# Moving x of chunk 1 and the v weights one wave earlier, with a newly searched order of steps, in a fused attention and MLP kernel

## The chip, the cores and the metric

One core of a Trainium2 chip. The metric is the device time of one launch in microseconds (us), lower is better. Profiles give a span that is about 2 us shorter than the time of the same run (201.3 and 203.08 us before, 204.6 and 206.41 changed). Every run is in the state that the records call fast. For one core the records also give the mean granted clock of TensorE (1.0 is full speed), which matters below.

## The reference

x has 2048 rows of 512. The block is: layer norm, q, k and v projections, attention of 32 heads of 16 over eight positions two apart (a row's own and seven earlier ones), an output projection with residual (this sum is h), layer norm of h, a gated MLP of 1376 hidden columns, and again a residual.

```python
off = jnp.arange(8) * 2
idx = pos[:, None] - off[None, :]            # each row looks at 8 rows, 2 apart
logits = jnp.einsum("bhsd,bhswd->bhsw", q, kg) * scale
attn = softmax(where(mask, logits, -1e9))
o = jnp.einsum("bhsw,bhswd->bhsd", attn, vg)
h = x + o @ wo
g = layernorm(h) @ W_gate
out = h + (g * (g > 0) * (layernorm(h) @ W_up)) @ W_down
```

## The kernel before

The rows are worked on in four chunks of 512 (chunk 0 to 3), which overlap. All steps are put in a list, and a table `RANK` gives each its place; each engine is given its steps in that order. The table was searched off the chip with assumed durations. The loads come first, in waves: a later wave is held back by a one-element copy on GpSimd that reads the earlier one and writes into the later one's tile (the first such copy runs at 3.61 us, and x of chunk 1 is issued at 3.81).

```python
for j in range(BPC):                                  # x of chunk 0: four blocks, on two queues
    (nc.scalar if j % 2 else nc.sync).dma_start(x_sm[:, j:j + 1, :], x_rows[:, j:j + 1, :])
for dt in range(NT):                                  # q and k weights: four slices, on two queues
    (nc.scalar if dt % 2 else nc.sync).dma_start(wqk_sb[:, dt:dt + 1, :], w3_r[:, dt:dt + 1, 0:2 * D])
# ... constants ...
nc.gpsimd.tensor_copy(out=x_sm[0:1, BPC, 0:1], in_=x_sm[0:1, 0, 0:1])          # gate
nc.sync.dma_start(x_sm[:, BPC:2 * BPC, :], x_rows[:, BPC:2 * BPC, :])           # x of chunk 1
nc.gpsimd.tensor_copy(out=wv_sb[0:1, 0, 0:1], in_=wqk_sb[0:1, NT - 1, 0:1])    # gate
nc.sync.dma_start(wv_sb[:], w3_r[:, :, 2 * D:3 * D])                            # v weights
nc.gpsimd.tensor_copy(out=x_sm[0:1, 2 * BPC, 0:1], in_=x_sm[0:1, BPC, 0:1])    # gate
# ... x of chunks 2 and 3, then wo, up, gate, down weights
```

Normalised rows are transposed before the products with the weights. Most are transposed on TensorE itself; those in `DMAT` by a DMA on the SP queue, one for each block of 128 rows: all four of x of chunk 3, two of h of chunk 1, all of h of chunks 2 and 3.

```python
DMAT = (('h',2,0),('h',2,2),('x',3,0),('x',3,2),('h',3,0),('h',3,2),('h',1,0))
# in layernorm(): xn is a normalised block
nc.sync.dma_start_transpose(out=dst.t[:, :, j * P:(j + 1) * P], in_=xn.t[:])
```

The sum over eight positions of attention times v is begun with a DMA too. After a v product on VectorE (128x4096, 2.2 us from start to start), an accumulating transfer of 512 KB, issued from GpSimd, adds its second half to its first. There are four of these in each of chunks 0, 1 and 2.

```python
def f_da(mt=mt):
    nc.gpsimd.dma_start(mt.t[:, 0:4, :], mt.t[:, 4:8, :], accum_op=ALU.add)
```

In the names used below, `xxn` is the normalising of one block of x on VectorE, `xtd` its transpose by DMA, `mu` a v product, `hxn` the normalising of a block of h.

The softmax here doesn't subtract the row's maximum and nothing guards it: scores larger than these inputs give would overflow.

Of the kernel before, what the change touches and what calls it, by code (L numbers as in the profile page):

```python
# [17 lines left out]
RANK = [  # L18
    0, 1, 2, 3, 4, 5, 6, 7, 8, 9, 10, 11, 12, 13, 14, 15, 16, 18, 19, 24,
    26, 31, 32, 17, 20, 22, 23, 25, 29, 34, 35, 28, 33, 37, 39, 41, 45, 48, 21, 27,  # L20
    30, 36, 38, 42, 44, 46, 63, 74, 40, 56, 68, 49, 51, 54, 43, 60, 72, 53, 66, 65,
    77, 70, 83, 75, 80, 90, 92, 87, 114, 102, 110, 85, 105, 93, 104, 115, 125, 129, 78, 88,
    95, 99, 103, 183, 193, 202, 132, 143, 150, 156, 152, 106, 109, 116, 123, 119, 168, 181, 216, 220,
    224, 180, 188, 217, 223, 231, 187, 196, 226, 229, 234, 162, 172, 201, 205, 207, 237, 240, 239, 245,
    247, 251, 242, 248, 243, 246, 252, 256, 259, 263, 250, 254, 265, 266, 272, 278, 269, 276, 285, 275,
    283, 273, 280, 286, 318, 322, 292, 301, 304, 314, 313, 324, 341, 311, 325, 298, 303, 334, 338, 326,
    330, 346, 354, 360, 337, 355, 317, 353, 347, 358, 370, 329, 352, 340, 348, 332, 345, 294, 350, 356,
    361, 374, 343, 365, 372, 381, 351, 362, 413, 357, 368, 367, 386, 418, 400, 425, 460, 464, 417, 427,
    457, 467, 376, 434, 446, 466, 410, 429, 437, 668, 55, 61, 52, 57, 50, 58, 47, 59, 62, 64,
    67, 84, 73, 82, 86, 71, 81, 69, 79, 89, 166, 175, 122, 136, 111, 130, 137, 190, 91, 101,  # L30
    127, 173, 149, 179, 94, 96, 163, 213, 158, 170, 98, 107, 108, 167, 208, 197, 249, 257, 244, 235,
    255, 260, 264, 268, 274, 296, 279, 302, 309, 305, 310, 307, 287, 295, 290, 293, 300, 319, 328, 364,
    369, 315, 320, 359, 363, 335, 342, 380, 382, 327, 336, 373, 375, 389, 395, 387, 392, 396, 402, 393,
    399, 398, 401, 397, 403, 405, 409, 404, 407, 411, 412, 416, 419, 420, 423, 421, 428, 422, 426, 431,
    474, 482, 441, 443, 458, 463, 453, 468, 483, 438, 448, 436, 452, 442, 451, 450, 454, 456, 488, 492,
    479, 498, 455, 487, 491, 500, 507, 461, 493, 445, 459, 481, 485, 471, 475, 496, 511, 539, 524, 533,
    520, 535, 526, 530, 541, 514, 540, 484, 502, 543, 544, 556, 581, 589, 538, 552, 559, 562, 549, 554,
    584, 587, 529, 547, 560, 564, 113, 120, 100, 124, 76, 117, 97, 112, 128, 133, 140, 144, 142, 146,
    164, 145, 154, 148, 157, 161, 209, 230, 174, 186, 198, 200, 195, 215, 182, 184, 199, 228, 189, 211,
    169, 177, 178, 194, 232, 241, 271, 281, 185, 191, 261, 253, 284, 297, 289, 282, 308, 312, 321, 331,  # L40
    339, 344, 378, 366, 377, 371, 379, 383, 385, 394, 388, 391, 390, 430, 439, 470, 490, 424, 432, 473,
    476, 440, 447, 486, 489, 406, 415, 465, 477, 501, 518, 497, 504, 508, 512, 494, 499, 521, 525, 517,
    519, 516, 522, 503, 505, 527, 528, 532, 546, 534, 537, 536, 548, 531, 542, 579, 597, 566, 594, 585,
    601, 561, 580, 609, 599, 603, 588, 592, 571, 575, 577, 600, 605, 606, 610, 595, 623, 602, 611, 582,
    614, 627, 558, 576, 574, 578, 568, 572, 565, 567, 583, 621, 648, 639, 645, 636, 649, 591, 616, 652,
    624, 635, 628, 633, 640, 655, 663, 665, 667, 632, 654, 661, 711, 650, 656, 707, 710, 644, 657, 659,
    669, 126, 138, 118, 134, 131, 139, 121, 135, 141, 147, 155, 160, 151, 171, 159, 165, 153, 176, 203,
    236, 218, 225, 192, 204, 214, 219, 258, 291, 262, 270, 222, 233, 267, 277, 227, 238, 212, 221, 288,
    316, 206, 210, 306, 299, 323, 333, 384, 349, 408, 414, 433, 435, 444, 462, 449, 506, 510, 509, 513,
    515, 469, 495, 478, 472, 480, 563, 570, 586, 593, 523, 551, 557, 569, 573, 590, 596, 598, 545, 550,  # L50
    553, 555, 615, 622, 604, 607, 612, 619, 608, 613, 626, 629, 618, 620, 630, 631, 617, 625, 634, 637,
    638, 641, 646, 653, 643, 651, 642, 647, 691, 695, 681, 692, 694, 698, 688, 697, 700, 679, 687, 674,
    677, 670, 680, 666, 671, 690, 673, 675, 672, 682, 658, 662, 660, 678, 683, 684, 689, 664, 685, 699,
    702, 676, 693, 705, 701, 706, 704, 709, 686, 703, 708, 713, 715, 716, 718, 696, 714, 719, 720, 722,
    724, 731, 712, 726, 732, 734, 717, 725, 727, 730, 728, 733, 735, 737, 721, 723, 729, 736,
]


# [33 lines left out]
class Plan:  # L92
# [9 lines left out]
    def add(self, key, *a, **k):  # L102
        op = Op(*a, **k)
        op.key = key
        op.seq = len(self.ops)
        if RANK:
            op.prio = RANK[op.seq]
        self.ops.append(op)
        for b in set(op.take) | set(op.use):
            b.left += 1  # L110
        return op
# [76 lines left out]
def kernel(  # L188
# [11 lines left out]
    nc = tc.nc  # L200
# [4 lines left out]
    NT = D // P  # L205
# [11 lines left out]
    BPC = CS // P  # L217
# [4 lines left out]
    x_rows = A_x.rearrange("b (tb p) d -> p (b tb) d", p=P)  # L222
# [20 lines left out]
    x_sm = sb.tile([P, NTB, D], BF16, name="x_sm")  # L243
    wqk_sb = sb.tile([P, NT, 2 * D], BF16, name="wqk_sb")
    wv_sb = sb.tile([P, NT, D], BF16, name="wv_sb")
# [32 lines left out]
    def setup():  # L278
# [3 lines left out]
            (nc.scalar if j % 2 else nc.sync).dma_start(x_sm[:, j:j + 1, :], x_rows[:, j:j + 1, :])  # L282
        for dt in range(NT):
            (nc.scalar if dt % 2 else nc.sync).dma_start(wqk_sb[:, dt:dt + 1, :], w3_r[:, dt:dt + 1, 0:2 * D])
        nc.scalar.preload_act_table_set("natural_log_exp_and_others")
        V.memset(warm[:], 0.0)
        make_identity(nc, identity[:])
# [7 lines left out]
        nc.gpsimd.memset(vT[:, :, 0:PADL], 0.0)  # L295


        nc.gpsimd.tensor_copy(out=x_sm[0:1, BPC, 0:1], in_=x_sm[0:1, 0, 0:1])
        nc.sync.dma_start(x_sm[:, BPC:2 * BPC, :], x_rows[:, BPC:2 * BPC, :])
        nc.gpsimd.tensor_copy(out=wv_sb[0:1, 0, 0:1], in_=wqk_sb[0:1, NT - 1, 0:1])  # L300
        nc.sync.dma_start(wv_sb[:], w3_r[:, :, 2 * D:3 * D])
        nc.gpsimd.tensor_copy(out=x_sm[0:1, 2 * BPC, 0:1], in_=x_sm[0:1, BPC, 0:1])
        for tk in range(2, NCK):
# [32 lines left out]
    DAL = 5.5  # L336
    TDD, TDL = 1.25, 1.5
    NWARM, NFILL = 44, 8
    DMAT = (('h',2,0),('h',2,2),('x',3,0),('x',3,2),('h',3,0),('h',3,2),('h',1,0))

    EARLY = (1, 2, 3)

# [20 lines left out]
    def load(t):  # L363
        return add(None, "LD", 0.0, None, lat=t)

    xload = [[load(t) for t in (3.4, 3.4, 4.2, 4.2)]] + [[load(t)] * BPC for t in (9.5, 14.0, 15.5)]
    wload = {n: load(t) for n, t in
             (("q", 8.0), ("k", 8.0), ("v", 12.0), ("o", 17.5), ("u", 21.5), ("g", 25.5), ("d", 29.5))}

    wb = Buf(bank_s)  # L370

# [14 lines left out]
    def layernorm(tk, src, dst_slots, pr, groups, on_act, residual=None):  # L386
# [7 lines left out]
        for grp in groups:  # L394
# [72 lines left out]
            for j0 in range(lo, hi, step):  # L467
                if (ln, tk, j0) in DMAT:
                    for j in range(j0, min(j0 + step, hi)):
# [38 lines left out]
    for tk in range(NCK):  # L508
# [143 lines left out]
        for t in range(NT):  # L652
# [18 lines left out]
            if (tk, t) in PESUM:  # L671
                u = Buf(od_s)
# [66 lines left out]
        for f0 in range(0, NFT, 2):  # L739
# [3 lines left out]
            for ft in fts:  # L743
# [20 lines left out]
                d = add(("ge%d" % (f0 // 2), tk), "ACT", A5, f_ge, [c], pr - 200, take=[gr], use=[gm], lat=AL)  # L764
# [50 lines left out]
    with tc.manual_schedule():  # L815
        setup()
        for op in todo:
            if op.fn is not None:
                op.fn()
# [35 lines left out]
```

## Time and profile before

| | before |
|---|---|
| time, first 3 runs | 204.51 us (204.45 to 204.53) |
| profiled run | 203.08 us, span 201.3 us |
| TensorE busy | 194.4 us, 97% |
| VectorE busy | 153.1 us, 76% |
| x of chunk 1 issued, landed | 3.81, 9.91 us |
| v weights issued, landed | 8.85, 13.38 us |

Timelines have the start in us, the busy time, engine and line, operation, output and inputs, count, and in brackets the idle time of the engine before the line with what ended it. SPq is the SP queue issuing a transfer. This is the view of waits of TensorE in the kernel before (what waited, for what, us in total, times, longest):

```profile
...
PE bank L525 <- DMA quad<-row: 0.7, 1, 0.7
...
PE bank L525 <- DMA wqk_sb<-in_A_wqkv_dram: 0.6, 1, 0.6
PE bank L750 <- DMA quad<-row: 0.4, 1, 0.4
```

`quad<-row` is a transposed block. TensorE waits once for those of x of chunk 3, once for those of h of chunk 1, and once for the q and k weights. Idle time is a little less than time lost, since the modelled end of the last matmul lies after the start of the next: the twelve v matmuls at 16.92 us count as 2.75 us busy, and the next group starts 2.59 us after their start. I therefore give lost time as the distance between two starts minus the work of the first (2.59 us for twelve is 0.216 us for one of 512 columns), as the prediction works it out.

### The profile page before, as it was taken

Reading aid. Unit: us, or ns where it says so; the run is one execution under the profiler, and the core shown is the slowest. Engines: PE = TensorE matmul, PEld = TensorE weight load, DVE = VectorE, ACT = ScalarE, POOL = GpSimd, SP = SyncE. Lnnn points to the kernel's source line nnn. Section 1 sums busy time; section 2 is a strip of 40 time slices with the busy share of each in tenths; the row PEclk is TensorE's granted clock in tenths of the full one; section 3 lists DMA queues with packets and bytes.
Section 4 is the critical chain, followed back from the end, with each engine's and each line's share of the span. In section 5 each row is a group of like instructions: output and inputs, shape, how many; then the busy total and the mean of one; then the engine's idle time right before and its main releaser. Section 6 shows DMA issues by size and latency. Waiting matters only on the chain.

```text
span 201.3 us, 2960 instructions
## 1 busy us (share of the span) xinstructions
PE 194.4 (97%) x1115; PEld 96.0 (48%) x1115; DVE 153.1 (76%) x239; ACT 121.9 (61%) x256; POOL 12.8 (6%) x29
## 2 busy tenths in 40 slices
PE   8799999989999999999999999999999999999993
PEld 8676445545445344434444444444444444444452
DVE  6778999999999999999995858799967412122313
ACT  3377699746899966787536679801566731277500
POOL 3000000420000013100122000000000000000000
PEclk9999999999999999999999999999999999999999
DMA  5799971896000008930299500131010050200103
GB/s 152 270 256 379 406 219 41 155 205 122 3 0 0 3 0 169 190 57 3 39 182 191 138 3 0 26 78 52 3 52 0 0 104 3 78 0 0 52 0 104
DMA packets 17676, 18.81 MB, mean 93 GB/s; under 512 B 8352, under 2 KB 14464, under 8 KB 17664
## 3 DMA queue, kind: packets, MB, share of 16 engines
q1 hardware_dynamic: 15360, 11.57, 18.7%
q0 software_dynamic: 1728, 6.29, 16.8%
q10 hardware_dynamic: 576, 0.79, 1.3%
q8 instruction: 8, 0.13, 0.3%
q14 instruction: 4, 0.03, 0.0%
HBM read 8.42 MB, written 2.10 MB: 52 GB/s over the span
## 4 chain that ended last, share of the span: by engine, by line
PE 55%; DVE 24%; DMA 11%; ACT 5%; issue 2%; SPq 1%; POOL 0%; DVEq 0%; ACTq 0%; POOLq 0%
PE bank L750 29%; PE bank L787 14%; DVE big L572 7%; DMA x_sm<-in_A_x_dram 7%; DVE big L660 7%; PE bank L525 6%; PE bank L712 5%; DMA quad<-row 4%; DVE st L420 2%; DVE row L455 2%; DVE gT L770 2%; DVE x_sm L723 1%; DVE big L663 1%; ACT big L645 1%; ACT row L409 1%
## 5 line engine op out<-in xcount | busy, mean ns | idle before, releaser
L750 PE MATMUL bank<-quad,wg_sb 128*128 128x512 bf16 (+1 forms) x176 | 42.5, 379 | 0.4 <-DMA quad<-row 0.4
L750 PE MATMUL bank<-quad,wu_sb 128*128 128x512 bf16 (+1 forms) x176 | 42.7, 379 | 0.1
L757 ACT ACTIVATE gr<-bank 128x512 bf16<-128x512 f32 (+1 forms) x44 | 25.4, 618 | 24.8 <-PE bank L750 23.0
L787 PE MATMUL bank<-wd_sb,gT 128*128 128x512 bf16 (+3 forms) x187 | 40.0, 367 | 0.0
L754 ACT CAST up_sb<-bank 128x512 bf16<-128x512 f32 (+1 forms) x44 | 25.1, 601 | 21.0 <-PE bank L750 19.3
L572 DVE TENSOR_TENSOR big<-quad,kT 128x4096 bf16<-128x4096 bf16 x16 | 36.2, 2283 | 0.1
L660 DVE TENSOR_TENSOR big<-big,vT 128x4096 bf16<-128x4096 bf16 x16 | 35.9, 2281 | 0.0
L770 DVE TENSOR_TENSOR gT<-gr,up_sb 128x1024 bf16<-128x1024 bf16 (+1 forms) x24 | 15.3, 642 | 24.0 <-ACT up_sb L754 14.4
L525 PE MATMUL bank<-quad,wqk_sb 128*128 128x512 bf16 (+1 forms) x144 | 30.6, 356 | 1.3 <-DMA quad<-row 0.7
L787 PEld LDWEIGHTS <-gT 128*128 128x128 bf16 (+1 forms) x187 | 18.1, 98 | 19.6 <-issue 0.4
L750 PEld LDWEIGHTS <-wg_sb 128*128 128x128 bf16 (+1 forms) x176 | 17.3, 100 | 21.3 <-issue 0.9
L750 PEld LDWEIGHTS <-wu_sb 128*128 128x128 bf16 (+1 forms) x176 | 17.5, 100 | 20.6 <-issue 0.7
L525 PEld LDWEIGHTS <-wqk_sb 128*128 128x128 bf16 x144 | 15.5, 114 | 13.5 <-issue 2.2
L798 DVE TENSOR_TENSOR row<-x_sm,bank 128x512 bf16<-128x512 bf16 (+1 forms) x17 | 10.6, 649 | 10.4 <-PE bank L787 10.4
L645 ACT CAST big<-bank 128x512 bf16<-128x512 f32 x32 | 17.8, 638 | 0.4 <-PE bank L639 0.4
L663 DVE TENSOR_TENSOR big<-big 128x1024 bf16<-128x1024 bf16 (+2 forms) x24 | 16.8, 728 | 0.1
L692 POOL DMA_DIRECT2D big<-big x12 | 10.5, 872 | 87.9 <-DVE big L660 59.8
L525 PE MATMUL bank<-quad,wv_sb 128*128 128x512 bf16 x64 | 15.7, 380 | 0.0
L712 PE MATMUL bank<-wo_sb,quad 128*128 128x512 bf16 x64 | 15.3, 379 | 0.0
L455 DVE TENSOR_SCALAR row<-x_sm,mv,rs 128x512 bf16<-128x512 bf16 x32 | 11.3, 407 | 3.1 <-ACT rs L437 3.1
L533 ACT CAST quad<-bank 128x512 bf16<-128x512 f32 x16 | 9.4, 609 | 4.5 <-PE bank L525 4.5
L500 ACT COPY quad<-bank 128x1024 bf16<-128x1024 bf16 (+1 forms) x9 | 8.0, 930 | 6.3 <-PE bank L484 6.2
(69 smaller groups left out, 146.7 us busy)
## 6 DMA issues: line engine op xcount, KB each, us to landing
big<-big POOLq DMA_DIRECT2D x12, 512.0 KB, 5.5
out_dram<-row SPq DMA_DIRECT2D x15, 128.0 KB, 1.8
x_sm<-in_A_x_dram SPq DMA_DIRECT2D x3, 512.0 KB, 6.1
wu_sb<-in_B_W_up_dram SPq DMA_DIRECT2D x1, 1376.0 KB, 9.7
wg_sb<-in_B_W_gate_dram SPq DMA_DIRECT2D x1, 1376.0 KB, 12.7
wd_sb<-in_B_W_down_dram SPq DMA_DIRECT2D x1, 1280.0 KB, 16.4
wqk_sb<-in_A_wqkv_dram ACTq DMA_DIRECT2D x2, 256.0 KB, 6.0
wqk_sb<-in_A_wqkv_dram SPq DMA_DIRECT2D x2, 256.0 KB, 6.2
```

Of the source, the lines that this page charges most:

```text
L455: V.tensor_scalar(out=xn.t[:], in0=x, scalar1=mv.t[:, j, 0:1], scalar2=rs.t[:, j:j + 1], op0=ALU.add if residual else ALU.subtract, op1=AL ...
L525: nc.tensor.matmul(mm.t[:, lo:hi], lhsT=wv_sb[:, dt, t:D:NT] if c == 2 else wqk_sb[:, dt, c * D + t:(c + 1) * D:NT], rhs=xnT.t[:, dt, lo:h ...
L572: V.tensor_tensor(out=pb.t[:].rearrange("p (t w) s -> p t w s", t=2), in0=q4, in1=k4, op=ALU.mult)
L645: nc.scalar.copy(out=ab.t[:, w, :], in_=bc.t[:])
L660: V.tensor_tensor(out=mt.t[:], in0=ab.t[:], in1=v8, op=ALU.mult)
L663: V.tensor_tensor(out=mt.t[:, 0:n, :], in0=mt.t[:, 0:n, :], in1=mt.t[:, n:2 * n, :], op=ALU.add)
L712: nc.tensor.matmul(od.t[:], lhsT=OT.t[:, t, j * P:(j + 1) * P], rhs=wo_sb[:, t, :], start=(t == 0), stop=(t == NT - 1 and tk not in RPE))
L750: nc.tensor.matmul(mm.t[:fs, :], lhsT=w_sb[:, dt, ft * P: ft * P + fs], rhs=hnT.t[:, dt, :], start=(dt == 0), stop=(dt == NT - 1))
L754: nc.scalar.copy(out=ub.t[:fs, i, :], in_=um.t[:fs, :])
L757: nc.scalar.activation(out=gr.t[:fs, i, :], in_=gm.t[:fs, :], func=ACT.Relu)
L770: V.tensor_tensor(out=gt.t[:fs, 0:n, :], in0=gr.t[:fs, 0:n, :], in1=ub.t[:fs, 0:n, :], op=ALU.mult)
L787: nc.tensor.matmul(od.t[:, c0:c1], lhsT=gts[ft].t[:fs, ft % 2, j * P:(j + 1) * P], rhs=wd_sb[:fs, ft, c0:c1], start=(ft == 0), stop=(ft == ...
```

## The change

The intent: have the input of chunk 1 sooner, and the v weights right behind it so that the DMA engines do not fall idle between the waves (88 GB/s from 9 to 11 us in the kernel before, 367 at 7.5), and let the search order all steps for these landing times.

```diff
@@ RANK: 738 places, 633 of them new (left out)
@@ setup()
         for dt in range(NT):
             (nc.scalar if dt % 2 else nc.sync).dma_start(wqk_sb[:, dt:dt + 1, :], ...)
+        nc.sync.dma_start(x_sm[:, BPC:2 * BPC, :], x_rows[:, BPC:2 * BPC, :])
         nc.scalar.preload_act_table_set("natural_log_exp_and_others")
 ...
-        nc.gpsimd.tensor_copy(out=x_sm[0:1, BPC, 0:1], in_=x_sm[0:1, 0, 0:1])
-        nc.sync.dma_start(x_sm[:, BPC:2 * BPC, :], x_rows[:, BPC:2 * BPC, :])
-        nc.gpsimd.tensor_copy(out=wv_sb[0:1, 0, 0:1], in_=wqk_sb[0:1, NT - 1, 0:1])
+        nc.gpsimd.tensor_copy(out=wv_sb[0:1, 0, 0:1], in_=x_sm[0:1, 0, 0:1])
         nc.sync.dma_start(wv_sb[:], w3_r[:, :, 2 * D:3 * D])
@@ assumed landing times for the search
-    xload = [[load(t) for t in (3.4, 3.4, 4.2, 4.2)]] + [[load(t)] * BPC for t in (9.5, 14.0, 15.5)]
+    xload = [[load(t) for t in (3.4, 3.4, 4.2, 4.2)]] + [[load(t)] * BPC for t in (8.5, 13.5, 15.0)]
-             (("q", 8.0), ("k", 8.0), ("v", 12.0), ...
+             (("q", 8.0), ("k", 8.0), ("v", 11.5), ...
```

`DMAT` has the same members in another sequence, which does nothing.

## The prediction

> **What bounds the kernel now.** I read the page first (busy shares, the 40 slices), then the timeline of TensorE for stretches that the waits name, then the timeline of the first 17 us on all engines, then the DMA share in half-microsecond windows.
>
> ```profile
> span 201.3 us, 2960 instructions
> PE 194.4 (97%) x1115; PEld 96.0 (48%) x1115; DVE 153.1 (76%) x239; ACT 121.9 (61%) x256; POOL 12.8 (6%) x29
> PE   8799999989999999999999999999999999999993
> DVE  6778999999999999999995858799967412122313
> ```
>
> TensorE has work nearly everywhere, and VectorE is as full as it from 12 to about 100 us. Since busy time of pipelined matmuls flatters, I measured the distance between starts. The twelve v matmuls of 512 columns that start at 16.92 are followed by the next group at 19.51, so a matmul takes 0.216 us and a group of four 0.865. Where the distance is longer, time is lost:
>
> ```profile
> 7.84 0.38 PE L525 MATMUL bank<-quad,wqk_sb 128*128 128x256 bf16 x2
> 8.82 0.41 PE L525 MATMUL bank<-quad,wqk_sb 128*128 128x256 bf16 x2 [0.60 <-DMA wqk_sb<-in_A_wqkv_dram]
> ...
> 39.60 1.03 PE L525 MATMUL bank<-quad,wqk_sb 128*128 128x512 bf16 x4
> 41.34 4.48 PE L525 MATMUL bank<-quad,wqk_sb 128*128 128x512 bf16 x20 [0.71 <-DMA quad<-row]
> ...
> 103.26 0.81 PE L787 MATMUL bank<-wd_sb,gT 128*128 128x512 bf16 x3
> 104.47 1.02 PE L750 MATMUL bank<-quad,wg_sb 128*128 128x512 bf16 x4 [0.40 <-DMA quad<-row]
> ```
>
> The first pair: 0.98 us for two matmuls of 256 columns (0.22 us), so 0.76 us lost to the q and k weights. The second: 1.74 us for 0.86 us of work, 0.88 us lost to the transposed rows of x of chunk 3. The third: 1.21 for 0.65, 0.56 us lost to transposed rows of h of chunk 1. Elsewhere from 9 us to the last matmul I find only 0.1 us at each switch between full and partial tiles, and two waits under 0.2 us at the broadcasts. So a change of loads and order has **about 1.4 us of lost TensorE time to win after 9 us**, 0.7% of the time, and 0.8 us before it. The work itself is not changed.
>
> The loads: x of chunk 1 is awaited here.
>
> ```profile
> 3.61 0.18 POOL L298 COPY x_sm<-x_sm 1x1 bf16<-1x1 bf16 x1 [1.17 <-DMA x_sm<-in_A_x_dram]
> 3.81 0.39 SPq L299 DMA_DIRECT2D x_sm<-in_A_x_dram  x1
> ...
> 8.85 0.37 SPq L301 DMA_DIRECT2D wv_sb<-in_A_wqkv_dram  x1
> ...
> 9.49 0.42 DVE L498 COPY quad<-bank 128x512 bf16<-128x512 bf16 x1 [1.10 <-PE bank L484]
> ...
> 9.93 2.47 DVE L420 BATCH_NORM_STATS2 st<-x_sm 128x6 f32<-128x512 bf16 x4
> ...
> 15.68 0.70 DVE L420 BATCH_NORM_STATS2 st<-x_sm 128x6 f32<-128x512 bf16 x1 [1.01 <-DMA x_sm<-in_A_x_dram]
> ```
>
> x of chunk 1 lands at 9.90 us (chain of waits: from 3.81, 6.09 us), v at about 13.4 (8.85 plus 4.5 to landing), x of chunk 2 at 15.65 (10.23 plus 5.42). Only the last holds VectorE, by 1.01 us. TensorE first wants v at 16.92 us, 3.5 us after it has landed: v is no wait today. In the half-microsecond windows the DMA runs at 367 GB/s at 7.5 us, then 98, 53, 84 and 117 GB/s from 9.0 to 11.0 us. That is the hole between the two waves.
>
> [...] the trace has VectorE idle 1.01 us for one load at 15.68. [...] x of chunk 1, queued on SP behind its q and k weights, lands 1.1 us after the last of those (8.8). [...] the trace has the fourth transposed row of chunk 3 landing at 41.21, 4.94 us after its issue, beside an accumulate issued at 35.44, where transposes have 2.5 us in the median.
>
> **The change part by part.**
> (a) x of chunk 1 loses its GpSimd gate. It is not issued with the weights for all that. In the built program it is the ninth load, takes the first load's completion semaphore, and still waits for that one (x block 1, issued 0.73, 2.7 us to landing, so about 3.4). Issue moves from 3.81 to about 3.4: **0.4 us**. [...] I put the landing at 9.4 to 9.9.
> (b) v's gate is now the first block of x (3.56) instead of the last q/k weight (8.65): issue at about 3.85, 5 us earlier, right behind x of chunk 1. It fills the hole: 0.5 MB at 370 GB/s is 1.4 us, landing about 11.3. TensorE gains nothing by that.
> (c) x of chunks 2 and 3 are still gated by x of chunk 1, but v is no longer ahead of them: about 13.5 and 15, some 2 us earlier, and the later weights with them (not awaited). The 1.01 us hole of VectorE closes; its first big product (16.38 today) then waits for ScalarE's copies of the four q/k groups of the first half. In the new order those are done at about 15.6 to 15.9, since the first statistics sit before them on ScalarE. VectorE's chain gains **0.5 to 0.8 us**.
> (d) The order. On VectorE one statistics step of chunk 1 moves ahead of the copy of the fourth transposed block of chunk 0. Today that copy ends at 9.91, and TensorE wants it at 10.83 (the copy of the third block on ScalarE ends at 10.73, just in time). With x at 9.9 it becomes 9.9 + 0.62 + 0.42 = 10.95: **0.1 to 0.2 us lost**; with x at 9.4, nothing.
> (e) On TensorE three more groups of chunk 2 (3 x 0.865 = 2.6 us) stand ahead of the first group of chunk 3: it is wanted at about 43.0 instead of 40.5. But the fourth row of chunk 3 is normalised only after two of the four big v products (2.2 us each), at about 36.9, so its transpose is issued near 37 and shares the engines with two accumulates. I put its landing at 41.5 to 43.5: of the 0.88 us, **0.5 to 0.9 us won**, mean 0.65.
> (f) The gap at 104: the two h rows of chunk 1 are again normalised right behind a v product whose accumulate goes out at the same time, and about the same TensorE work (36 down-projection matmuls, one score group, one denominator) covers it. I leave it at 0.56, plus or minus 0.4.
> (g) The rest keeps the same matmuls. For h of chunk 2 the order puts two v products, not one, before the rows, 2.3 us later, but its output projection comes 1.7 us earlier and 0.9 us more work covers it. Margin today: rows at 134.98 (last transpose), wanted at 137.3. I see no new wait there. The tail is as it was.
> Sum on TensorE: +0.1 (d), -0.65 (e), 0 (f), 0 (g), so about **-0.5 us on 204.51: 204.0 us**. What VectorE gains in (c) counts only where TensorE waits for it.
>
> **Rivals.**
> 1. *The whole slack is won.* Landing times were right, both holes at 40 and 104 close and the copies are never late: -1.4 us and a bit of the broadcast waits, 203.0. For it: the order was searched for such times. Against: the search has a fixed latency for a transpose, and the trace shows 4.94 us beside an accumulate against 2.5.
> 2. *The first wave is too full.* x of chunk 1 and v take bandwidth from the q/k weights, which TensorE awaits at 8.82. If the last weight slips by 1 us, all slips by 1 us, and x with it, which then also blocks VectorE in front of the copy: +1 to +1.5, 205.7. [...]
> 3. *A new wait in place of the one removed.* The fourth transposed row lands after 44, or h of chunk 1 meets its accumulate worse: +0.5 to +1 over my sum, about 204.8. What I know least.
> 4. *VectorE is the true bound to 100 us.* Its chain of products is gapless from 16 to 100, and the output projections at 52.6 and 90.7 start within 0.1 to 0.6 us of its last step before them. Then the gain of TensorE at 40 is only kept as far as VectorE gained, 0.5 to 0.8 us: the same size, so 204.0 to 204.3.
>
> **Range and chances.** Rival 1 gives 203.0, rivals 3 and 2 give 204.8 and 205.7; I take 203.0 to 205.3. Two per cent is 4.1 us: nothing in the trace has so much to give (1.4 + 0.8 in all), and to lose it a load would have to slip by 4 us. Faster 0.02, same 0.95, slower 0.03.
>
> **What would show it right or wrong.** Right: x of chunk 1 issued at 3.4 and landing by 9.9; v issued at 3.9; no DMA hole at 9 to 11; no 1 us wait of VectorE near 15; the wait for transposed rows near 43 under 0.4 us; a wait near 104 still there; the q/k wait at 8.8 within 0.2. Wrong: q/k weights later than 9.2, a wait of TensorE for VectorE's copy at 10.8 over 0.3, or new waits for transposed rows near 137 or 171.

## The result, and the profile after

| | before | changed |
|---|---|---|
| median | 204.28 us (203.67 to 204.53, 6 runs) | 207.41 us (205.74 to 208.54, 6 runs) |
| ratio | | 1.0148, 95% interval 1.0099 to 1.0197 |
| profiled run | 203.08 us, span 201.3 | 206.41 us, span 204.6 |
| granted clock of the runs | 1.0 (profiled run) | 1.0 in two (205.74, 206.41), 0.992 in four (207.02 to 208.54) |

A ratio is the mean time of one kernel's fast runs over that of the other's of the same rounds, so it is not quite the ratio of the medians. The change costs 1.5%: inside the 2% band, but clearly on the slow side and 2.1 us above the range of the prediction. The times also scatter more than those of before.

The same view of waits, changed kernel (its lines are one lower in the file, so L524 is L525 of before):

```profile
PE bank L524 <- DMA quad<-row: 2.6, 1, 2.6
...
PE bank L749 <- DMA quad<-row: 1.0, 1, 1.0
...
PE bank L524 <- DMA wqk_sb<-in_A_wqkv_dram: 0.9, 1, 0.9
...
PE bank L524 <- DVE quad L497: 0.2, 1, 0.2
```

Neither of the two waits for transposed blocks is gone: both are longer. (Left out is, among others, a wait that ends the warm-up matmuls and sets nothing.) In lost time, from the distances between starts:

| TensorE waits for | before, at | changed, at | difference |
|---|---|---|---|
| transposed x of chunk 3 | 0.88, 40.3 us | 2.78, 43.3 us | +1.90 |
| transposed h of chunk 1 | 0.56, 103.7 | 1.16, 106.0 | +0.60 |
| copy of the fourth block of chunk 0 | 0, 10.8 | 0.32, 11.0 | +0.32 |
| q and k weights | 0.76, 8.0 | 1.06, 7.9 | +0.30 |
| sum | | | +3.1 |

The spans differ by 3.3 us. So in these two profiles nearly all of the difference is waits of TensorE, and the largest is the one that I expected to shrink. The timeline around it:

```profile
32.19 8.70 SPq L472 DMA_TRANSPOSE quad<-row  x4
...
34.95 1.01 POOL L691 DMA_DIRECT2D big<-big  x1 [24.40 <-DVE big L659]
...
36.48 0.40 DVE L454 TENSOR_SCALAR row<-x_sm,mv,rs 128x512 bf16<-128x512 bf16 x1
...
37.12 0.86 POOL L691 DMA_DIRECT2D big<-big  x1 [1.17 <-DVE row L454]
...
46.32 3.62 PE L524 MATMUL bank<-quad,wqk_sb 128*128 128x512 bf16 x15 [2.62 <-DMA quad<-row]
```

and the chain that ended last, same stretch (start, us, what):

```profile
36.91 1.82 SPq L472
...
38.77 7.42 DMA quad<-row
```

where the kernel before has

```profile
34.95 1.26 SPq L473
...
36.27 4.94 DMA quad<-row
```

The late block is normalised at 36.48 to 36.88, behind two v products, as predicted. But its transpose, issued at 36.91, is not the last: another follows at 38.77 and lands at 46.19. The four transposes are issued at 32.19, 33.54, 36.91 and 38.77, and land at 34.71, 36.08, 42.30 and 46.19. The third in the queue's order is the late block. The fourth, whose block had been ready since about 32, stood behind it. The packets in the trace show the rest. From 36.5 to 39.0 us only the 4096-byte packets of the first accumulate move (128 of about 0.35 us each, and the DMA share is 0.89 or more of the 16 engines in each half microsecond). From 39.0 to 40.5 the 512 packets of the third transpose (256 bytes) pass. Then the second accumulate has nearly all of the engines' time, and only from 42.5 to 44.0 do the 512 of the fourth transpose pass. Its last packets, 32 of four bytes, come one by one beside the next accumulate, and it counts as landed at 46.19. **In this stretch, with the next accumulate already queued, one transpose got through between two of them** (512 packets each time), and the new order had left two on the wrong side. (Near 103 us of the kernel before the next accumulate was issued only at 102.72, and two got through, 1024 packets from 102 to 104 us.)

### The profile page after: what moved, and what is told of

The parts are those of the page before. It is cut to its first block, busy times and chain, and to the rows that moved or that the text cites. A ratio compares the mean times of both kernels' runs of the same rounds, so it can differ in the third digit from the quotient of the medians.

```text
span 204.6 us, 2949 instructions
## 1 busy us (share of the span) xinstructions
PE 192.9 (94%) x1095; PEld 95.2 (47%) x1115; DVE 152.2 (74%) x239; ACT 123.0 (60%) x256; POOL 12.7 (6%) x28
## 4 chain that ended last, share of the span: by engine, by line
PE 68%; DVE 17%; DMA 11%; issue 2%; SPq 1%; DVEq 0%
PE bank L749 29%; PE bank L524 14%; PE bank L786 14%; DVE big L659 7%; DMA quad<-row 6%; PE bank L711 5%; DMA x_sm<-in_A_x_dram 5%; DVE big L571 3%; PE bank L577 3%; DVE gT L769 2%; DVE big L662 1%; DVE x_sm L722 1%; PE bank L483 1%; DVE row L454 1%; PE bank L638 1%
## 5 line engine op out<-in xcount | busy, mean ns | idle before, releaser
L786 PE MATMUL bank<-wd_sb,gT 128*128 128x512 bf16 (+3 forms) x181 | 39.2, 366 | 0.4 <-DVE row L454 0.2
L753 ACT CAST up_sb<-bank 128x512 bf16<-128x512 f32 (+1 forms) x44 | 25.6, 600 | 20.5 <-PE bank L749 8.9
L524 PE MATMUL bank<-quad,wqk_sb 128*128 128x512 bf16 (+1 forms) x139 | 30.0, 356 | 3.9 <-DMA quad<-row 2.6
L524 PEld LDWEIGHTS <-wqk_sb 128*128 128x128 bf16 x144 | 15.3, 114 | 16.2 <-issue 4.6
L524 PE MATMUL bank<-quad,wv_sb 128*128 128x512 bf16 x62 | 15.7, 379 | 0.1
L722 DVE SCALAR_TENSOR_TENSOR x_sm<-x_sm,bank 128x512 bf16<-128x512 bf16 x12 | 8.1, 682 | 5.9 <-PE bank L711 5.9
L419 DVE BATCH_NORM_STATS2 st<-x_sm 128x6 f32<-128x512 bf16 x16 | 10.4, 672 | 2.3 <-DMA x_sm<-in_A_x_dram 2.3
```

What stands on the lines that cost most here:

```text
L524: nc.tensor.matmul(mm.t[:, lo:hi], lhsT=wv_sb[:, dt, t:D:NT] if c == 2 else wqk_sb[:, dt, c * D + t:(c + 1) * D:NT], rhs=xnT.t[:, dt, lo:h ...
L753: nc.scalar.copy(out=ub.t[:fs, i, :], in_=um.t[:fs, :])
L786: nc.tensor.matmul(od.t[:, c0:c1], lhsT=gts[ft].t[:fs, ft % 2, j * P:(j + 1) * P], rhs=wd_sb[:fs, ft, c0:c1], start=(ft == 0), stop=(ft == ...
```

## The experiments

Fourteen runs, of twelve new kernels, the changed kernel once more, and one of the twelve once more; those of one letter ran on one chip beside the same runs of the kernel before. All results were correct. `step(engine, name, chunk, n)` is the n-th step of that name in the engine's order; a changed `prio` moves it.

**Which half of the change costs the time?** a1_loads is the changed kernel with the old table:

```diff
-RANK = [ ...new... ]
+RANK = [ ...as before... ]
```

> The new loads with the old order of steps. Theory T (the order did it: two transposed rows of chunk 3 queue behind accumulates, TensorE loses 2.8 us at 43 us instead of 0.9 at 40): within 0.6 us of before, 204.0 to 204.9, the wait near 40 still about 0.9 and no longer one; q/k weights may land 0.2 to 0.3 later. Rival L (the loads did it, by slower q/k weights and x of chunk 1): over 205.5, with the loss before 12 us.

Measured: 203.34 us against 203.40, ratio 0.9988 (0.9964 to 1.0012). TensorE loses 0.79 us at 40 and 0.46 at 103. For the new loads alone neither a cost nor a gain is shown (the interval leaves room for 0.4% of gain and 0.1% of cost). a2_order is the other half, the kernel before with the new table.

> The old loads with the new order. Theory T: the wait for transposed rows near 43 is 2 to 3.5 us again, time 206.5 to 208, some runs with granted clock 0.992. Rival L: 204 to 205.

Measured: 207.61 us, ratio 1.0181 (1.0148 to 1.0213). The loss is in the order, all of it. Its transposes land at 42.63 and 46.54, and three of its six runs have a granted clock of 0.988 to 0.992. The profiled run is one of those (0.988), and shows what that is. View of stretches of time, a2_order (busy us and count by engine, then PEclk, DMA share, GB/s):

```profile
44.00:46.00 2.00, 0.00 (x0) 0.00 (x0) 1.86 (x5) 2.00 (x5) 0.00 (x0) 1.00 1.11 215
46.00:48.00 2.00, 1.32 (x6) 0.72 (x7) 2.00 (x2) 0.91 (x2) 0.00 (x0) 0.96 1.03 203
48.00:50.00 2.00, 2.00 (x6) 0.73 (x5) 2.00 (x6) 0.00 (x0) 0.00 (x0) 0.50 0.37 72
```

TensorE does nothing from 44 to 46 us (the distance of starts is 3.35 us), comes back at full clock, and is at half clock from 47.85 to 51.26: matmuls there start 0.427 us apart instead of 0.216. 3.41 us at half rate are 1.7 us of work lost.

The clock records show when. The half clock lasts 3.41 us here and in d1_after_again, and the stretches of full clock around it (40.96 and 153.6 us here) are 12 and 45 times that; in the profiles of the kernel before and of the changed one, whose only drop comes after the last matmul, the full clock before it lasts 197.97 and 201.39 us, 58 and 59 times. So I divide these traces into windows of 3.41 us, counted back from a drop. The window at whose end the clock fell had 2.2 us without a matmul here and 2.5 in d1_after_again (by the modelled ends of the matmuls). In the profile of the changed kernel, which shows no drop there, the windows (counted back from the drop at 205.49 us) cut the wait in two, 1.4 and 1.3 us. In that of the kernel before, the clock did not fall at the end of the window with the last matmul (1.7 us without one), but one window later, at 203.06. What lies between 1.7 and 2.2 us is not shown. In d1_after_again 2.97 us between two starts were followed by the drop, in the changed kernel 2.99 were not: in these two traces the place of the windows goes with the difference, the length of the wait does not. (The drops at 203.06 and 205.49 find no matmul to slow. That such drops are also why other profiled runs have mean clocks of 0.996 to 1.0 is my estimate.)

**Which step of the order?** a3_sp exchanges two transposes on the SP queue of the changed kernel and nothing else:

```diff
+    a, b = step("SP", "xtd", 3, 2), step("SP", "xtd", 3, 3)
+    a.prio, b.prio = b.prio, a.prio
     todo = plan.order()
```

> The changed kernel with only two transposes of chunk 3 exchanged on the SP queue, so that the row that is normalised late goes last and holds up no other. Theory T: only one transpose is left behind an accumulate, it lands near 42, TensorE wants it at 43.5: the wait of 2.8 us is gone, time 203.6 to 204.8, granted clock 1.0 in all runs. Rival V (VectorE is the true bound, the wait only hides its lateness): at most 1 us won, 205.5 or more, the same time lost at the output projection of chunk 0 near 53.

Measured: 203.74 us, ratio 1.0031 (0.9996 to 1.0065). The third transpose now lands at 38.11 and the late one at 42.26, before TensorE wants it at 43.5, and the wait is gone:

```profile
40.00:46.00 6.00, 6.00 (x29) 3.12 (x29) 5.76 (x7) 4.77 (x10) 1.37 (x2) 1.00 1.09 208
```

(The changed kernel has 3.71 us of TensorE in this stretch.) From a ratio of 1.0148 to 1.0031 is 2.4 us for two steps exchanged (the two ratios are from different submissions, each against the kernel before). One of the six runs (205.68 us) still had a clock of 0.992; it was not the profiled one, and why is open. a4_dve cures the same thing from the other side:

```diff
+    step("DVE", "xxn", 3, 3).prio = step("DVE", "mu3", 0).prio - 0.5
```

> The changed kernel with only the late normalisation step of chunk 3 put ahead of the v products. Theory T: as the run before, all four rows are ready by 32.5, last one lands near 41.3, no wait at 43, 203.6 to 204.8. Rival V: 205.5 or more.

Measured: 204.87 us, ratio 1.0067 (1.0044 to 1.0089), 0.1 over the range that I gave. The last transpose lands at 38.95 and there is no wait at 43. But the v products come later, and TensorE loses 0.52 us at the output projection near 52.7, which waits for VectorE. Rival V is right in part: VectorE is close behind TensorE there.

**Are the accumulates what holds the transposes up?** b2_noacc lets VectorE do the first two of chunk 0:

```diff
-    DACC = tuple((k, t) for k in range(3) for t in range(4))
+    DACC = tuple((k, t) for k in range(3) for t in range(4) if k or t in (0, 2))
```

> The changed kernel with the first two accumulating transfers of chunk 0 done by VectorE instead (2 x 1.2 us more of VectorE, and the late row some 1.2 us later). Theory A (the accumulates hold the transposes up): the third and fourth transpose issue near 38 and 39.4 and land 2.5 us later, near 40.6 and 42, no wait at 43, time 203.5 to 205. Rival S (the transposes are slow by themselves or by their late issue): they still take over 4 us and the wait stays over 1.5 us.

Measured: 205.30 us, ratio 1.0120 (1.0072 to 1.0167), 0.3 over the range. The mechanism is as expected. The late block and the one behind it are issued at 38.05 and 39.28, later than in the changed kernel, and land at 40.48 and 41.77, in 2.4 and 2.5 us; no wait at 43. The time goes elsewhere, since VectorE has 2.4 us more to do:

```profile
PE bank L711 <- DVE quad L666: 0.9, 1, 0.9
```

This line is the output projection waiting for VectorE (1.08 us lost near 52.6); the wait for h of chunk 1 loses 1.41 us instead of 1.16. So theory A holds for the transposes, and VectorE is the next bound.

**What does the low clock cost?** b1_keep puts 44 idle matmuls where TensorE waits:

```diff
+    def f_keep():
+        for _ in range(44):
+            nc.tensor.matmul(wf.t[:, 0:P], lhsT=warm[:], rhs=warm[:], start=True, stop=True)
+    keep = Op("PE", 0.056 * 44, f_keep, [], first.prio - 0.5, take=[wf], lat=PEL)   # first: first group of chunk 3
```

> The changed kernel with 44 idle matmuls of 128 columns (2.46 us) on TensorE just ahead of the first group of chunk 3, where it waits. The transposed rows still land near 46.2, so no time of the wait itself is won. Theory C (the wait of about 3 us lets the clock drop to half for some 3 us in part of the runs): granted clock about 1.0 in all runs, spread under 1 us, median 205.5 to 206.6 where the changed kernel has 205.7 to 208.5. Rival N (the spread has another cause): clock 0.992 and over 207 in about half of the runs as before.

Measured: median 206.32 us, ratio 1.0163 (1.0122 to 1.0203), clock 0.996 to 1.0 in all six runs, but a spread of 1.5 us. The clock behaves as theory C says; the ratio to before was no better than that of the changed kernel in another submission. So both ran once more, side by side:

> The changed kernel once more, on the same chip as the next run. Theory C: some runs with granted clock 0.988 to 0.992, these 1.5 us slower than those with 0.996 to 1.0; median 3 us over before. Rival N: times do not go with the clock.

Measured: median 206.51 us, ratio 1.0139 (1.0092 to 1.0186). Two runs at a clock of 0.992 took 208.35 and 208.31 us; the four at 1.0 took 205.77 to 206.82.

> b1_keep once more on the same chip: idle matmuls in the wait. Theory C: no run under 0.995, mean lower than d1_after_again by 1.7 us times the share of its runs with the low clock, so 0.5 to 1.2 us. Rival N: the same mean as d1_after_again within 0.4 us.

Measured: median 206.63 us, ratio 1.0141 (1.0108 to 1.0174), clock 0.996 to 1.0. The mean is only 0.26 us under that of d1, short of the 0.5 to 1.2 expected and within the 0.4 that rival N allowed: the clock went as theory C says, the time did not. What is shown: over both submissions the changed kernel had the low clock in 6 of 12 runs, mean 207.97 us, and 206.14 in the others, a difference of 1.8; with idle matmuls in the wait, none of 12 runs had it. What is not shown is a gain: those 12 runs have a mean of 206.49 us, 0.35 above the full-clock runs of the changed kernel. The idle matmuls seem to cost most of what they save; how is open.

**The smaller losses.** b3_sp_tv adds to a3_sp the old place of the copy of the fourth block:

```diff
+    step("DVE", "xtv3", 0).prio = step("DVE", "xst", 1).prio - 0.5
```

> As a3_sp, and the copy of the fourth transposed block of chunk 0 put back ahead of the first statistics step of chunk 1 on VectorE. Theory: the two small waits of TensorE near 11 us in a3_sp (0.35 and part of the next) go, 0.3 us less than a3_sp: 203.2 to 203.6. Rival: the wait is on ScalarE's copy instead and nothing is won.

Measured: 203.41 us, ratio 1.0012 (0.9975 to 1.0050). The wait at 11 us is gone from the profile; in time the difference to a3_sp is too small to be shown. In the changed kernel that wait reads, from the timeline:

```profile
10.34 0.70 DVE L419 BATCH_NORM_STATS2 st<-x_sm 128x6 f32<-128x512 bf16 x1 [1.98 <-DMA x_sm<-in_A_x_dram]
...
10.95 0.41 DVE L497 COPY quad<-bank 128x512 bf16<-128x512 bf16 x1
...
11.41 5.39 PE L524 MATMUL bank<-quad,wqk_sb 128*128 128x256 bf16 x31 [0.16 <-DVE quad L497]
```

VectorE stands 1.98 us at a load that it could have waited for later, with a copy that TensorE wants right behind. b4_sp_tv_h1 adds that the blocks of h of chunk 1 are normalised ahead of the v product of chunk 2, so that their transposes go ahead of its accumulate:

```diff
+    m = step("DVE", "mu3", 2).prio
+    for n in range(4):
+        step("DVE", "hxn", 1, n).prio = m - 0.5 + 0.1 * n
```

> As b3_sp_tv, and the four normalised rows of h of chunk 1 put ahead of the v product of chunk 2, so that their transposes are issued before its accumulate. Theory A: the two transposes land 2.5 us after issue, the wait of 1.15 us near 103 goes, 202.3 to 202.8. Rival: VectorE idles 1.2 us for the scale, its chain comes 2.5 us later and TensorE waits as long at the output projection of chunk 2 near 118.

Measured: 202.29 us against 203.18, ratio 0.9976 (0.9928 to 1.0025). That is the changed kernel with all three repaired, no longer slower than before, and not shown to be faster. The timeline of the changed kernel at this place:

```profile
101.16 0.86 POOL L691 DMA_DIRECT2D big<-big  x1 [16.48 <-DVE big L659]
...
101.25 3.97 SPq L472 DMA_TRANSPOSE quad<-row  x2
```

and of b4_sp_tv_h1:

```profile
96.34 2.50 SPq L472 DMA_TRANSPOSE quad<-row  x2
...
99.74 0.86 POOL L691 DMA_DIRECT2D big<-big  x1 [19.10 <-DVE big L659]
```

In the first, accumulate and transposes go out together, and the second transpose, issued at 102.54, lands at 107.23. In the second, both transposes (issued 96.34 and 97.62) have landed by 98.75 and 100.06, and TensorE does not wait.

**A better version?** The same reading, applied to the kernel before, says that its two waits for transposed blocks can be closed by order alone. c1_loads_h1 (new loads, old table) moves the rows of h of chunk 1, and the last two products of gate and up of chunk 0, ahead of the v product of chunk 2:

```diff
+    m = step("DVE", "mu3", 2).prio
+    step("DVE", "gu4", 0).prio, step("DVE", "gu5", 0).prio = m - 0.7, m - 0.6
+    for n in range(4):
+        step("DVE", "hxn", 1, n).prio = m - 0.5 + 0.1 * n
```

> New loads, old order, with one change: on VectorE the two last products of gate and up of chunk 0 and the four normalised rows of h of chunk 1 go ahead of the v product of chunk 2. Theory A: the two transposes are issued before the accumulate, land 2.5 us after issue, and the wait near 103.5 (0.46 in a1_loads) goes: 0.4 to 0.5 us under before. Rival: VectorE's 1.2 us idle for the scale comes back as a wait of TensorE at 118, the same time as before.

Measured: 203.06 us against 202.52, ratio 1.0020 (0.9975 to 1.0065). The wait near 103 is gone from the profile, but the 0.4 to 0.5 us expected are not there: no gain in time is shown. c2_loads_h1_pe also gives TensorE two groups of chunk 2 ahead of the first of chunk 3:

```diff
+    step("PE", "qkv2", 3).prio = step("PE", "qkv2", 2).prio + 0.5
```

> As c1, and on TensorE the first group of chunk 3 two groups (1.7 us) later. Theory: the wait of 0.8 near 40 goes too; the output projection of chunk 0 can start at the earliest when VectorE's last step for it is done, near 51.5, so 0.5 to 0.8 of it is kept: 1.0 to 1.3 us under before. Rival V: VectorE takes it back near 52, 0.4 under before like c1.

Measured: 202.37 us, ratio 0.9969 (0.9926 to 1.0011): unclear, and less than expected. c4_old_h1_pe makes the same two changes of order with the old loads, so it is the kernel before with seven steps moved:

> The two changes of order of c2 with the old loads. Theory: TensorE is the bound, so the loads matter only where VectorE's 0.7 us are wanted, at the output projection of chunk 0: 0.7 to 1.1 us under before, 0.2 to 0.5 more than c2. Rival: the same as c2, the new loads are worth nothing.

Measured: 201.70 us, ratio 0.9942 (0.9905 to 0.9978), the only version whose interval lies wholly below 1 (one of fourteen such comparisons, so it wants a repeat). Its view of waits of TensorE has none for `quad<-row` left:

```profile
...
PE bank L484 <- DVE row L455: 1.0, 1, 1.0
PE bank L525 <- DMA wqk_sb<-in_A_wqkv_dram: 0.8, 1, 0.8
```

I had expected it to be behind c2 by 0.2 to 0.5; it is ahead by 0.7 in the medians, with overlapping intervals. The new loads are not shown to help, or to hurt.

**Does v, right behind, delay x of chunk 1?** c3_loads_vlate is a1_loads with the old gate of v:

```diff
-        nc.gpsimd.tensor_copy(out=wv_sb[0:1, 0, 0:1], in_=x_sm[0:1, 0, 0:1])
+        nc.gpsimd.tensor_copy(out=wv_sb[0:1, 0, 0:1], in_=wqk_sb[0:1, NT - 1, 0:1])
```

> New loads and old order, but v gated by the last q/k weight as in the kernel before: only x of chunk 1 is moved. Theory B (v right behind x of chunk 1 takes the DMA engines that are done early and so delays its last pieces): x of chunk 1 lands at 9.5 to 9.8 where the runs with the new loads have 10.2 to 10.6 mostly. Rival: 10.1 or later, what sets it is the q/k weights ahead of it. Time within 0.5 of before either way.

Measured: 203.37 us, ratio 1.0025 (0.9978 to 1.0073). x of chunk 1 lands at 9.85, near what theory B said, but the q and k weights were early in this run too, the last at 8.54. The distance from the last weight to x is 1.31 us here, 1.27 in the changed kernel, 1.36 in a1_loads, 1.13 in the kernel before. Theory B is not supported by this one profile: x follows the weights, by 1.1 to 1.5 us in all sixteen profiles, and with the new loads the last weight lands anywhere from 8.1 to 9.7 us. (The three profiles with the old loads have 8.8 to 9.0.)

## Why the prediction was wrong

The prediction was 204.0 us, 203.0 to 205.3. It has the sign wrong, and the time is outside.

- **The bound** (TensorE, with 1.4 us to win after 9 us) fits what was measured. a1_loads moves the loads and leaves TensorE's waits, and the time stays. c4_old_h1_pe closes both waits and wins 1.2 us (0.58% of its reference), though c2_loads_h1_pe, with both closed too, is not clear of noise.
- **(a) failed by little.** The issue moved from 3.81 to 3.35, as worked out. "I put the landing at 9.4 to 9.9": it was 10.31. It followed the last q and k weight by 1.27 us, and that weight came 0.26 us later than before (9.04 instead of 8.78).
- **(b) was right, (c) in its direction.** v was issued at 3.86 and landed at 11.61; the DMA hole at 9 to 11 us is filled (307 GB/s instead of 88), and x of chunk 2 lands at 14.14 instead of 15.66. VectorE's first big product starts at 15.96 instead of 16.29, 0.33 us earlier where I said 0.5 to 0.8 (15.62 in a1_loads). None of it is time, as TensorE was not waiting for it.
- **(d)** said 0.1 to 0.2 us; it was 0.32, because x came later than I put it.
- **(e) is the step that failed.** "I put its landing at 41.5 to 43.5: of the 0.88 us, 0.5 to 0.9 us won." Instead 1.90 us were lost, 2.55 away from my term of -0.65. Two things were wrong in it. I took the late block for the last in the SP queue; it is the third, and a finished block stands behind it. That was there to be read in the order of the built program. The late block itself landed at 42.30, inside my range; the one behind it, at 46.19, is what TensorE waited for. And I took the engines as shared between transposes and accumulates. At 36 to 44 us of the changed kernel they mostly were not: no packet of the third transpose moved until the accumulate ahead of it had ended, at 39.0, and with the next one queued only that transpose passed between the two. a3_sp shows the first (exchange the two, and 2.4 us are back; the late block then lands at 42.26), b2_noacc that the accumulates are what holds them up (without them, 2.4 to 2.5 us to landing), and the packets how.
- **(f)** said 0.56, plus or minus 0.4; it was 1.16. The rows came 1.9 to 2.3 us later, but TensorE wanted them 2.3 us later too. What had changed is that their transposes went out together with the accumulate, and took 5.64 and 4.69 us to land instead of 4.80 and 3.51. b4_sp_tv_h1 shows that they collide: ahead of it, they take 2.4 us.
- **(g) was right.** No new wait near 137 or 171.
- **Not in the sum at all: the clock.** In 6 of 12 runs the mean clock was 0.992, and these took 1.8 us more (207.97 against 206.14); in the one of them that was profiled, d1_after_again, the clock fell to half for 3.41 us after this wait of 3 us. That is why the scatter grew. The range had no term for a wait that costs more than its length.
- **Rival 3** ("the fourth transposed row lands after 44, or h of chunk 1 meets its accumulate worse") was what happened, both halves of it, and I gave it +0.5 to +1. I had called it what I know least, and should have followed the queue's order to the end before sizing it. **Rival 2** was wrong in its mechanism: the 0.3 us later weights of the changed profile are also in a2_order with the old loads, where 1.06 us are lost to them, and in b1_keep with the new ones only 0.18 are: the weights scatter from run to run. **Rival 4** shows in a4_dve and b2_noacc: VectorE is the next bound near 52 us.

## What to carry to other kernels

When a new order moves a step, follow it through every queue behind it, the DMA queue too: one late item at the wrong place can hold up finished work (here a block ready at about 32 us was issued at 38.77 and landed at 46.19). Do not price a small transfer beside a large one by sharing; look in the trace whether it waits for the end of the large one, and issue it first (here the changed kernel's transposes beside accumulates of 512 KB took 4.7 to 7.4 us to land, against a median of 2.5, and 2.4 in b4_sp_tv_h1, issued ahead). A change of loads is worth only what the bounding engine waits for (here nothing that is shown: ratio 0.9988 for a1_loads), and a single wait of about 3 us on TensorE can cost more than its length, through the clock (here 1.8 us more in 6 of 12 runs; where the clock fell in a profile, 2.2 us or more of the wait lay in one window of 3.41 us).
